# LSH attention with a soft MoE on one core: slot maxima joined by a reduce, and a new table of places

## The chip, the core and the metric

The kernel runs on one core of a Trainium2 chip. The metric is the device time of one execution in microseconds (us); of several runs the median counts. Before the change it is 492.49 us, the median of 3 runs (492.34 to 494.26).

## What is computed

```python
def _attn_ref(q, k, v, proj):                      # q, k, v: 4 x 8 x 768 x 64, proj: 64 x 6
    q_bits = (np.einsum('bhsd,dk->bhsk', q, proj) > 0)
    k_bits = (np.einsum('bhsd,dk->bhsk', k, proj) > 0)
    ...
    mask = q_bucket[:, :, :, None] == k_bucket[:, :, None, :]
    scores = np.where(mask, scale * np.matmul(q, k.transpose(0, 1, 3, 2)), -1e9)
    scores = scores - np.max(scores, axis=-1, keepdims=True)
    attn = np.exp(scores)
    attn = attn / (np.sum(attn, axis=-1, keepdims=True) + 1e-09)
    return np.matmul(attn, v)

def _moe_ref(x, phi, w1, w2):                      # x: 3072 x 512, 8 experts of 4 slots
    logits = x @ phi
    d = np.exp(logits - logits.max(0, keepdims=True))
    d /= d.sum(0, keepdims=True) + 1e-09
    slot_input = d.T @ x
    ...
    for e in range(E):
        slot_out[e] = np.maximum(slot_input[e] @ w1[e], 0.0) @ w2[e]
    c = np.exp(logits - logits.max(1, keepdims=True))
    c /= c.sum(1, keepdims=True) + 1e-09
    return c @ slot_out
```

The output of the attention, 4 batches of 768 rows with 8 heads side by side, is the x of the MoE. The softmax of its dispatch runs over all 3072 rows, so a running maximum and a running sum of each of the 32 slots go from batch to batch.

## The kernel before

There are 32 heads (4 batches of 8). Of each head, TensorE makes the raw scores twice. `smax` (L692) multiplies queries and keys for the row maxima, which VectorE takes from PSUM with `most` (L701, L704: 9 reductions of 128x512 a head) and turns into a shift (`shift`, L730 to L733) that a transpose and a small DMA put into the matrix XY (`shift_rows`, L740, L743, L600). `scores` (L755) then gives shifted scores, ScalarE makes exponents of them (`exps`, L761), GpSimd (POOL in the profile) adds the exponents up (`acc`, L769, L772), and TensorE multiplies them by v (`av`, L782: 24 matmuls a head, v from `load_v`, L578).

Two heads share one pair of loads (`load`, L484). Each pair is split into a rounded part on ScalarE (`split_hi`, L592, L609) and a rest on VectorE (`split_lo`, L596, two TENSOR_TENSOR of 128x768 a pair, both inputs in SBUF). The parts go to XY by DMAs of SyncE's queue (`spread_y`, `spread_bits`, `spread_l`, `spread_x`, all L600). The MoE's weights (w, L474, L476) come in by the same queue.

After the 8th head of a batch come its steps for the MoE. `batch_both` (L893 on ScalarE, L895 twice on GpSimd) adds two halves of the logits; `batch_max` (L906 to L914 on VectorE) makes the maximum of each slot over the batch; `batch_exp`, `batch_turn` and `batch_slots` (L961, 48 matmuls) weigh the rows; `batch_weigh` and `batch_share` (L995 to L1006) make the other softmax. In `batch_max` the tile `ml` has 64 partitions that matter: L906 takes each partition's maximum over 384 columns, L908 copies each half of 32 partitions beside the other, L909 joins the two, and L910 doubles the result to the partitions from 64 on.

The order is written by hand: tables give each step of each head a place. WHEN holds the places of an ordinary pair of heads, FIRST and LAST those at the two ends. A place is counted in slots, six to a head; steps are issued in order of their places, and each engine and each queue then takes its own instructions strictly in that order. All `batch_` steps have their places in WHEN as well, except for the last batch's.

What the change touches is these three tables and `batch_max`.

Of the kernel before, what the change touches and what calls it, by code (L numbers as in the profile page):

```python
# [76 lines left out]

FIRST = {('bits', 0): -69.9775,
 ('first_x', 0): -30.1551,
 ('first_x', 1): -25.0682,  # L80
 ('first_x', 2): -20.412,
 ('first_x', 3): -18.4961,
 ('load', 4, 0): -3.5217,
 ('load', 4, 1): -4.0427,
 ('bits', 2): -14.3602,
 ('split_hi', 2): -6.1587,
 ('split_lo', 2, 0): -4.0091,
 ('split_lo', 2, 1): -3.1985,
 ('spread_y', 2): -4.0649,
 ('spread_bits', 2): -3.553,  # L90
 ('spread_l', 2): 7.1875,
 ('spread_x', 2): 2.0822,
 ('smax', 1, 0, 0): -15.9674,
 ('smax', 1, 0, 1): -11.9944,
 ('smax', 1, 1, 0): -10.2152,
 ('smax', 1, 1, 1): -15.7053,
 ('smax', 1, 2, 0): -4.3906,
 ('smax', 1, 2, 1): -4.1302,
 ('smax', 1, 3, 0): -3.9981,
 ('smax', 1, 3, 1): -7.967,  # L100
 ('smax', 1, 4, 0): -3.8293,
 ('smax', 1, 4, 1): -5.0023,
 ('smax', 1, 5, 0): -4.8646,
 ('smax', 1, 5, 1): -9.7674,
 ('first_y', 1): -54.5168,
 ('first_y', 2): -17.6137,
 ('spread_y', 1): -27.3342,
 ('spread_l', 0): -18.6619,
 ('spread_bits', 1): -21.1518,
 ('bits_rest',): -37.973,  # L110
 ('bits_copy', 0): -66.7928,
 ('bits_copy', 1): -56.5144,
 ('first_w', 0, 0): -66.5811,
 ('first_w', 0, 1): -45.7928,
 ('copy_ident',): -27.8207,
 ('bits_out',): -12.7699,
 ('shift_first', 0): -19.1938,
 ('rows_first', 0): -18.4864,
 ('shift_first', 1): -13.5686,
 ('rows_first', 1): -12.6498,  # L120
 ('most', 1, 0): -13.0129,
 ('most', 1, 2): -10.1579,
 ('most', 1, 3): -12.9853,
 ('most', 1, 4): -3.8181,
 ('most', 1, 6): -3.2633,
 ('most', 1, 7): -6.0805,
 ('most', 1, 8): -3.0814,
 ('most', 1, 10): -4.6253,
 ('most', 1, 11): -9.4308,
 ('bits_first', 1): -46.476,  # L130
 ('split_hi', 0): -80.2217,
 ('split_lo', 0, 0): -30.0379,
 ('split_lo', 0, 1): -20.3056,
 ('spread_x', 0): -11.7196,
 ('load_v', 0): -22.952,
 ('smax', 0, 0, 0): -39.3574,
 ('scores', 0, 0, 0): -14.2041,
 ('most', 0, 0): -28.4376,
 ('exps', 0, 0): -11.531,
 ('smax', 0, 0, 1): -32.3847,  # L140
 ('scores', 0, 0, 1): -9.483,
 ('smax', 0, 1, 0): -31.1779,
 ('scores', 0, 1, 0): -8.3933,
 ('most', 0, 2): -23.5522,
 ('exps', 0, 2): -7.5483,
 ('smax', 0, 1, 1): -56.6523,
 ('scores', 0, 1, 1): -1.1034,
 ('most', 0, 3): -51.1186,
 ('exps', 0, 3): -0.8554,
 ('smax', 0, 2, 0): -33.7433,  # L150
 ('scores', 0, 2, 0): -12.1245,
 ('most', 0, 4): -25.3553,
 ('exps', 0, 4): -10.2628,
 ('smax', 0, 2, 1): -25.6195,
 ('scores', 0, 2, 1): -5.5845,
 ('smax', 0, 3, 0): -25.5483,
 ('scores', 0, 3, 0): -1.2874,
 ('most', 0, 6): -19.4151,
 ('exps', 0, 6): 1.0484,
 ('smax', 0, 3, 1): -26.0166,  # L160
 ('scores', 0, 3, 1): 0.5805,
 ('most', 0, 7): -23.0552,
 ('exps', 0, 7): 1.0692,
 ('smax', 0, 4, 0): -18.3291,
 ('scores', 0, 4, 0): -10.0448,
 ('most', 0, 8): -14.3729,
 ('exps', 0, 8): -7.9213,
 ('smax', 0, 4, 1): -23.8505,
 ('scores', 0, 4, 1): -4.5738,
 ('smax', 0, 5, 0): -21.0143,  # L170
 ('scores', 0, 5, 0): -2.6163,
 ('most', 0, 10): -18.7244,
 ('exps', 0, 10): -0.999,
 ('smax', 0, 5, 1): -20.7774,
 ('scores', 0, 5, 1): 1.5881,
 ('most', 0, 11): -17.8201,
 ('exps', 0, 11): 3.2827,
 ('av', 0, 0): -4.211,
 ('acc', 0, 1): 0.5901,
 ('av', 0, 1): 1.0472,  # L180
 ('acc', 0, 2): 3.7833,
 ('av', 0, 2): 2.6287,
 ('acc', 0, 3): 8.0943,
 ('av', 0, 3): 4.1871,
 ('acc', 0, 4): 9.2872,
 ('av', 0, 4): 4.819,
 ('acc', 0, 5): 12.8178,
 ('av', 0, 5): 9.3332,
 ('spread_l', 1): -14.0544,
 ('spread_x', 1): -13.7504,  # L190
 ('load_v', 1): -44.3971,
 ('scores', 1, 0, 0): 4.973,
 ('exps', 1, 0): 6.1018,
 ('scores', 1, 0, 1): 3.4362,
 ('scores', 1, 1, 0): 3.7635,
 ('exps', 1, 2): 4.5791,
 ('scores', 1, 1, 1): 3.0982,
 ('exps', 1, 3): 5.7775,
 ('scores', 1, 2, 0): 2.917,
 ('exps', 1, 4): 5.8263,  # L200
 ('scores', 1, 2, 1): 9.7364,
 ('scores', 1, 3, 0): 10.4691,
 ('exps', 1, 6): 10.964,
 ('scores', 1, 3, 1): 5.8015,
 ('exps', 1, 7): 8.512,
 ('scores', 1, 4, 0): 5.3574,
 ('exps', 1, 8): 6.9816,
 ('scores', 1, 4, 1): 10.0245,
 ('scores', 1, 5, 0): 11.0987,
 ('exps', 1, 10): 12.5989,  # L210
 ('scores', 1, 5, 1): 8.2291,
 ('exps', 1, 11): 10.001,
 ('shift', 1): 0.0971,
 ('shift_rows', 1): 0.888,
 ('av', 1, 0): 10.6213,
 ('acc', 1, 1): 12.6345,
 ('av', 1, 1): 10.7441,
 ('acc', 1, 2): 13.2627,
 ('av', 1, 2): 11.6349,
 ('acc', 1, 3): 15.0399,  # L220
 ('av', 1, 3): 11.8759,
 ('acc', 1, 4): 19.4341,
 ('av', 1, 4): 14.7303,
 ('acc', 1, 5): 19.5025,
 ('av', 1, 5): 15.0341,
 ('load', 2, 0): -29.7899,
 ('load', 2, 1): -48.8868,
 ('load_v', 2): 14.3982,
 ('smax', 2, 0, 0): -0.6141,
 ('scores', 2, 0, 0): 11.2906,  # L230
 ('most', 2, 0): 1.9018,
 ('exps', 2, 0): 11.4754,
 ('smax', 2, 0, 1): 1.3301,
 ('scores', 2, 0, 1): 16.8442,
 ('smax', 2, 1, 0): 2.1038,
 ('scores', 2, 1, 0): 17.3813,
 ('most', 2, 2): 4.5992,
 ('exps', 2, 2): 17.9432,
 ('smax', 2, 1, 1): 3.4166,
 ('scores', 2, 1, 1): 13.5684,  # L240
 ('most', 2, 3): 6.6254,
 ('exps', 2, 3): 13.9228,
 ('smax', 2, 2, 0): 5.3372,
 ('scores', 2, 2, 0): 13.5443,
 ('most', 2, 4): 6.8467,
 ('exps', 2, 4): 16.2233,
 ('smax', 2, 2, 1): -0.0995,
 ('scores', 2, 2, 1): 11.5208,
 ('smax', 2, 3, 0): 1.5951,
 ('scores', 2, 3, 0): 12.5714,  # L250
 ('most', 2, 6): 2.9705,
 ('exps', 2, 6): 13.4436,
 ('smax', 2, 3, 1): 3.1284,
 ('scores', 2, 3, 1): 12.9678,
 ('most', 2, 7): 6.2017,
 ('exps', 2, 7): 14.722,
 ('smax', 2, 4, 0): 2.6343,
 ('scores', 2, 4, 0): 17.8316,
 ('most', 2, 8): 4.6871,
 ('exps', 2, 8): 17.9065,  # L260
 ('smax', 2, 4, 1): 5.4192,
 ('scores', 2, 4, 1): 15.908,
 ('smax', 2, 5, 0): 5.9488,
 ('scores', 2, 5, 0): 16.8341,
 ('most', 2, 10): 7.5949,
 ('exps', 2, 10): 17.5487,
 ('smax', 2, 5, 1): 7.6679,
 ('scores', 2, 5, 1): 16.4966,
# [1072 lines left out]
```

## Time and profile before

| what | value |
|---|---|
| median of 3 runs | 492.49 us |
| the profiled execution | 493.42 us, its span 491.8 us |
| instructions | 10961 |
| granted TensorE clock, mean | 0.979 of full speed |

The profile is of one execution. Its page gives for each engine the busy time, for each stretch the busy share and the granted clock of TensorE (2.4 GHz is 1.0, 1.2 GHz is 0.5), the chain of work that ended last, and groups of instructions by line. The queries on the trace give single instructions in order of time, with the idle time in front of each and what ended it in square brackets. PE is TensorE, DVE VectorE, ACT ScalarE, POOL GpSimd, SPq the queue of DMAs that SyncE issues.

### The profile page before, as it was taken

To read this page: it belongs to the slowest core of one execution; us is meant where nothing else is said; L and a number is where in the kernel's file an instruction comes from. 1 tells how busy PE (TensorE), PEld (TensorE's weight loads), DVE (VectorE), ACT (ScalarE), POOL (GpSimd) and SP (SyncE) were. 2 spreads that over 40 slices of the span, in tenths; PEclk is the share of its full clock that TensorE was granted. 3 is DMA by queue.
4 is the path that set the end of the run, shared out by engine and by line. 5 is a ranking of instruction groups with operands and counts; after the bars stand their busy time and mean duration, and the time that the engine had idled before them with its cause. 6 is when DMAs were issued, how large, how long until landed. Compare 5 with 4: busy or idle time off the path is not lost.

```text
span 491.8 us, 10961 instructions
## 1 busy us (share of the span) xinstructions
PE 455.0 (93%) x4159; PEld 286.3 (58%) x4159; DVE 374.0 (76%) x680; ACT 271.7 (55%) x569; POOL 332.7 (68%) x209
## 2 busy tenths in 40 slices
...
GB/s 181 168 151 141 126 224 143 212 135 229 136 221 59 179 178 181 175 181 178 182 124 112 188 142 202 164 194 100 170 43 155 46 163 319 365 379 301 413 361 258
DMA packets 37703, 93.20 MB, mean 190 GB/s; under 512 B 7106, under 2 KB 13380, under 8 KB 37652
## 3 DMA queue, kind: packets, MB, share of 16 engines
...
q14 instruction: 18, 0.15, 0.1%
...
HBM read 52.76 MB, written 6.29 MB: 120 GB/s over the span
## 4 chain that ended last, share of the span: by engine, by line
PE 65%; DMA 13%; DVE 9%; SPq 8%; issue 2%; ACT 1%; DVEq 0%; ACTq 0%
PE st L755 22%; PE av L782 15%; PE smx L692 12%; SPq L600 7%; DMA v<-vt 6%; DMA XY<-w 5%; PE qs L1255 3%; PE qh L1202 3%; DVE ml L909 3%; DVE mx L704 2%; DVE w L596 2%; PE mi L794 2%; PE mi L639 2%; PE mi L819 1%; ACT w L592 1%
## 5 line engine op out<-in xcount | busy, mean ns | idle before, releaser
L772 POOL TENSOR_TENSOR acc<-acc,pt 128x768 f32<-128x768 f32 x125 | 236.4, 1900 | 42.6 <-ACT pt L761 37.6
L761 ACT ACTIVATE pt<-st 128x512 f32<-128x512 f32 x288 | 156.9, 591 | 50.0 <-PE st L755 44.4
L755 PE MATMUL st<-XY 128*128 128x256 f32 (+1 forms) x768 | 176.6, 347 | 0.1
L704 DVE TENSOR_REDUCE mx<-smx 128x1 f32<-128x512 f32 x192 | 129.6, 687 | 36.1 <-PE smx L692 35.3
L782 PE MATMUL av<-pt,v 128*32 128x384 f32 x1536 | 135.3, 488 | 6.1 <-DMA v<-vt 4.6
L755 PEld LDWEIGHTS st<-XY 128*128 128x128 f32 x768 | 126.7, 194 | 20.9 <-issue 5.3
L692 PE MATMUL smx<-XY 96*128 96x256 f32 (+1 forms) x384 | 120.2, 367 | 18.1 <-DVE mx L704 14.4
L692 PEld LDWEIGHTS smx<-XY 96*128 96x128 f32 x384 | 69.5, 195 | 46.0 <-DVE mx L704 22.1
L782 PEld LDWEIGHTS av<-pt,v 128*32 128x32 f32 x1536 | 46.9, 110 | 79.0 <-issue 62.6
L701 DVE TENSOR_REDUCE mx<-smx 128x2 f32<-128x512 f32 x96 | 65.9, 687 | 5.9 <-PE smx L692 4.9
L769 POOL TENSOR_TENSOR acc<-pt 128x768 f32<-128x768 f32 x32 | 58.8, 1837 | 9.2 <-ACT pt L761 5.3
L786 ACT COPY avs<-av 128x384 f32<-128x384 f32 x32 | 15.4, 481 | 59.4 <-PE av L782 59.4
L596 DVE TENSOR_TENSOR w<-raw,w 128x768 fp32r<-128x768 f32 x28 | 37.8, 1351 | 9.9 <-ACT w L592 9.8
L592 ACT CAST w<-raw 128x768 fp32r<-128x768 f32 x30 | 23.7, 833 | 12.6 <-DMA XY<-mr 5.3
L609 ACT CAST XY<-w 64x768 fp32r<-64x768 f32 x30 | 23.5, 833 | 0.1
L797 ACT ACTIVATE sm<-mi,eps 128x384 f32<-128x384 f32 x15 | 8.7, 582 | 19.9 <-PE mi L794 19.9
L842 DVE TENSOR_TENSOR xq<-mi,r 128x384 f32<-128x384 f32 x30 | 16.7, 558 | 2.2
L841 DVE STREAM_TRANSPOSE mi<-avs 128x384 f32<-128x384 f32 x30 | 17.6, 586 | 0.5
L895 POOL TENSOR_TENSOR dl<-lacc,dl 64x384 f32<-64x384 f32 x6 | 7.8, 1304 | 14.2 <-issue 14.0
L996 POOL TENSOR_TENSOR lacc<-sm,cm 128x192 f32<-128x192 f32 x3 | 1.5, 510 | 23.1 <-DVE cm L995 23.1
L1255 PE MATMUL qs<-w 128*32 128x128 f32 x464 | 15.5, 274 | 0.4 <-issue 0.4
L811 ACT COPY r<-rt 64x12 f32<-64x12 f32 x60 | 12.0, 200 | 6.2 <-DVE rt L803 5.5
(174 smaller groups left out, 366.3 us busy)
## 6 DMA issues: line engine op xcount, KB each, us to landing
...
```

What stands on the lines that cost most here:

```text
L592: nc.scalar.copy(st[h]["w4"][:, 2 * x], st[h]["raw", x])
L596: (nc.vector if h > 2 else nc.gpsimd).tensor_tensor(out=w[:, 2 * x + 1], in0=st[h]["raw", x], in1=w[:, 2 * x], op=ALU.subtract)
L600: eng.dma_start(out=dst.bitcast(F32), in_=src.bitcast(F32))
L692: nc.tensor.matmul(pt[:, o:o + b - a], s["Y"][0:96, 0, t * P:(t + 1) * P], s["Y"][0:96, 1, a:b], start=True, stop=True)
L701: nc.vector.tensor_reduce(out=mx[:, n - 1:n + 1], in_=s["sm_ps", n - 1].rearrange("p (a x) -> p a x", a=2), axis=AX.X, op=ALU.max)
L704: nc.vector.reduce_max(out=mx[:, n:n + 1], in_=s["sm_ps", n], axis=AX.X)
L755: nc.tensor.matmul(pt[:, o:o + b - a], x[:, 1, i * P:(i + 1) * P], x[:, 0, a:b], start=first, stop=not first)
L761: nc.scalar.activation(s["P", n // 4][:, 512 * u:512 * u + 512], s["st_ps", n - (n % 4 == 2)], AF.Exp, scale=D ** -0.5)
L769: nc.gpsimd.tensor_tensor(out=s["acc"], in0=pr[:, 0:S], in1=pr[:, S:2 * S], op=ALU.add)
L772: eng.tensor_tensor(out=s["acc"], in0=s["acc"], in1=pr[:, a * S:(a + 1) * S], op=ALU.add)
L782: nc.tensor.matmul(s["av"][2 * e + 32 * c:2 * e + 32 * c + 32, 0:HC], s["v"][:, i, e:e + 32], pr[:, o + c * HC:o + (c + 1) * HC], start=(i ...
L1255: nc.tensor.matmul(pos[i][32 * j:32 * j + 32, 0:w], hTs[g][:, f, 32 * j:32 * j + 32], wt[1, x, 2 * g + f // 4, j][:, (f % 4) * HM + o:(f % ...
```

## The change

In `batch_max` the tile `ml` gets a fourth column, the first result goes to column 0 (`mo`), its copy from the other half to column 1 (`sw`), and L909 becomes a TENSOR_REDUCE over these two neighbouring columns instead of a TENSOR_TENSOR of one column with the other. All numbers of the tables are new, so all steps have other places; no step is added or left out.

```diff
-WHEN = {'load': -21.761,
- 'bits': -14.953,
- 'bits_over': -14.2535,
- 'split_hi': -12.6082,
- 'split_lo': [-11.9997, -11.2616],
- 'spread': [[-11.7311, -11.8254, -10.8277, -7.598], [-10.8259, -11.7635, -11.5808, -10.4552]],
- 'load_v': [0.1314, 2.3531],
...
- 'av': [[8.8176, 9.1545, 9.4692, 9.5265, 9.5397, 9.7898], [5.9962, 6.0054, 6.1722, 6.2052, 6.3699, 6.3882]],
...
- 'batch_both': 23.58,
- 'batch_max': 25.0983,
...
+WHEN = {'load': -17.7191,
+ 'bits': -14.4811,
+ 'bits_over': -14.4231,
+ 'split_hi': -11.8329,
+ 'split_lo': [-11.0358, -8.8327],
+ 'spread': [[-11.1688, -7.9572, -7.1212, -4.9753], [-9.4418, -9.0048, -8.9766, -8.3581]],
+ 'load_v': [0.8254, 0.8377],
...
+ 'av': [[9.338, 9.6759, 9.8253, 9.848, 9.9231, 9.9801], [6.073, 6.1257, 6.303, 6.4394, 6.7221, 7.1612]],
...
+ 'batch_both': 21.828,
+ 'batch_max': 24.3,
...
     def batch_max(b):
         z = bst[b]
-        ml = dp.tile([P, 3], F32, name="ml", bufs=1)
-        mb, sw, z["lb"] = (ml[:, n:n + 1] for n in range(3))
+        ml = dp.tile([P, 4], F32, name="ml", bufs=1)
+        mo, sw, mb, z["lb"] = (ml[:, n:n + 1] for n in range(4))
         z["al"] = dp.tile([P, 1], F32, name="al", bufs=1)
         z["nm"], z["om"] = run_n[b % 2], run_n[1 - b % 2]
-        nc.vector.reduce_max(out=mb[0:64], in_=logits_of(b)[0:64], axis=AX.X)
+        nc.vector.reduce_max(out=mo[0:64], in_=logits_of(b)[0:64], axis=AX.X)
         for x in range(2):
-            nc.vector.tensor_copy(sw[32 * x:32 * x + 32], mb[32 - 32 * x:64 - 32 * x])
-        nc.vector.tensor_tensor(out=mb[0:64], in0=mb[0:64], in1=sw[0:64], op=ALU.max)
+            nc.vector.tensor_copy(sw[32 * x:32 * x + 32], mo[32 - 32 * x:64 - 32 * x])
+        nc.vector.reduce_max(out=mb[0:64], in_=ml[0:64, 0:2], axis=AX.X)
         nc.vector.tensor_copy(mb[64:128], mb[0:64])
```

What the new tables do is seen in the order on the engines. The first place is VectorE at the end of the first batch, around `batch_max` (L906 to L912). Of the names, smx are raw scores in PSUM, w the split pair, raw its load, ml the maxima. Before:

```order
L704 TENSOR_REDUCE mx<-smx 128x1
L596 TENSOR_TENSOR w_1701<-raw_1481,w_1701 128x768
L704 TENSOR_REDUCE mx<-smx 128x1 x2
L596 TENSOR_TENSOR w_1701<-raw_1483,w_1701 128x768
L841 STREAM_TRANSPOSE mi<-avs 128x384
L842 TENSOR_TENSOR xq<-mi,r 128x12x32
L906 TENSOR_REDUCE ml<-dl 64x1
L908 COPY ml<-ml 32x1 x2
L909 TENSOR_TENSOR ml<-ml 64x1
L910 COPY ml<-ml 64x1
L912 TENSOR_SCALAR run_n_124<-ml 128x1
L704 TENSOR_REDUCE mx<-smx 128x1
```

And with the change:

```order
L704 TENSOR_REDUCE mx<-smx 128x1
L906 TENSOR_REDUCE ml<-dl 64x1
L908 COPY ml<-ml 32x1 x2
L909 TENSOR_REDUCE ml<-ml 64x1
L910 COPY ml<-ml 64x1
L912 TENSOR_SCALAR run_n_124<-ml 128x1
L704 TENSOR_REDUCE mx<-smx 128x1
L596 TENSOR_TENSOR w_1718<-raw_1497,w_1718 128x768
L704 TENSOR_REDUCE mx<-smx 128x1
L841 STREAM_TRANSPOSE mi<-avs 128x384
L842 TENSOR_TENSOR xq<-mi,r 128x12x32
L596 TENSOR_TENSOR w_1718<-raw_1499,w_1718 128x768
```

`batch_max` now stands ahead of both L596, and the second L596 stands behind L841 and L842 instead of ahead of them, in this pair and in the others.

The second place is SyncE's queue of DMAs in one ordinary pair of heads. XY<-w, XY<-bt and XY<-mr are the parts, bits and shifts that go to XY, v_103 is the v of the pair's second head. Before:

```order
L484 DMA raw_1187<-qk 128x768
L484 DMA raw_1189<-qk 128x768
L474 DMA w<-w 128x1024
L600 DMA XY_152<-mr 1x12x128
L600 DMA XY_153<-w_1113 64x2x768
L600 DMA XY_153<-w_1113 32x2x768
L600 DMA XY_151<-bt 13x384 x2
L600 DMA XY_151<-bt 12x384 x2
L600 DMA XY_151<-w_1113 32x2x768
L600 DMA XY_151<-w_1113 64x2x768 x2
L600 DMA XY_151<-w_1113 32x2x768
L578 DMA v_103<-vt 128x384
```

And with the change:

```order
L484 DMA raw_1203<-qk 128x768
L484 DMA raw_1205<-qk 128x768
L578 DMA v_103<-vt 128x384
L600 DMA XY_152<-mr 1x12x128
L600 DMA XY_153<-w_1126 64x2x768
L600 DMA XY_153<-w_1126 32x2x768
L600 DMA XY_151<-w_1126 64x2x768
L600 DMA XY_151<-bt 13x384 x2
L600 DMA XY_151<-bt 12x384 x2
L600 DMA XY_151<-w_1126 32x2x768
L600 DMA XY_151<-w_1126 64x2x768
L600 DMA XY_151<-w_1126 32x2x768
```

The load of v_103 went from behind the shift and the ten transfers to XY to ahead of all of them, and the weight piece (w<-w) that stood ahead of the shift went elsewhere.

## Rows read from the trace of the kernel before

**Rows 1.** The page: busy time of each engine, share of the span, instructions.

```profile
PE 455.0 (93%) x4159; PEld 286.3 (58%) x4159; DVE 374.0 (76%) x680; ACT 271.7 (55%) x569; POOL 332.7 (68%) x209
```

**Rows 2.** Stretches: length, busy time by engine, granted clock; first ordinary pairs, then batch pairs.

```profile
core 0: us, PE busy (x) PEld busy (x) DVE busy (x) ACT busy (x) POOL busy (x), PEclk, DMA share, GB/s
64.88:89.06 24.18, 23.11 (x192) 14.42 (x192) 20.66 (x37) 15.21 (x32) 18.93 (x10) 1.00 0.69 185
...
89.06:114.14 25.08, 24.36 (x199) 15.24 (x197) 20.91 (x38) 15.09 (x32) 18.92 (x10) 1.00 0.65 171
...
138.33:169.77 31.44, 27.32 (x246) 17.23 (x245) 28.34 (x52) 17.30 (x40) 21.21 (x17) 0.89 0.53 141
169.77:194.69 24.92, 24.41 (x202) 15.24 (x204) 20.50 (x36) 15.09 (x32) 21.46 (x11) 1.00 0.65 174
...
243.06:275.02 31.96, 27.12 (x241) 17.20 (x234) 28.38 (x50) 17.67 (x41) 21.21 (x18) 0.89 0.52 141
275.02:300.97 25.95, 24.69 (x205) 15.08 (x208) 22.19 (x37) 15.21 (x32) 21.72 (x13) 1.00 0.64 166
300.97:326.34 25.37, 23.86 (x198) 14.54 (x194) 20.55 (x36) 15.07 (x32) 18.92 (x10) 1.00 0.68 184
...
350.75:381.65 30.90, 25.95 (x240) 16.13 (x233) 28.25 (x50) 17.53 (x41) 21.13 (x17) 0.94 0.42 104
```

**Rows 3.** Line L909: durations in ns, least, median, most.

```profile
L909 DVE TENSOR_TENSOR ml<-ml x4: 150/4286/4301, 143.4 to 439.5; 64x1 f32<-64x1 f32 x4
```

**Rows 4.** Timeline of VectorE at the end of the first batch: start, us, what.

```profile
142.54 0.53 DVE L906 TENSOR_REDUCE ml<-dl 64x1 f32<-64x384 f32 x1
...
143.44 4.30 DVE L909 TENSOR_TENSOR ml<-ml 64x1 f32<-64x1 f32 x1
147.77 0.15 DVE L910 COPY ml<-ml 64x1 f32<-64x1 f32 x1
```

**Rows 5.** Timeline of GpSimd there: the run, and its first instruction alone.

```profile
142.36 9.15 POOL L772 TENSOR_TENSOR acc<-acc,pt 128x768 f32<-128x768 f32 x5
142.36 1.84 POOL L772 TENSOR_TENSOR acc<-acc,pt 128x768 f32<-128x768 f32 x1
```

**Rows 6.** Timeline of TensorE: its first matmul after L909, in three batches.

```profile
148.76 0.80 PE L692 MATMUL smx<-XY 96*128 96x512 f32 x1 [4.12 <-DVE mx L704]
253.53 0.80 PE L692 MATMUL smx<-XY 96*128 96x512 f32 x1 [4.30 <-DVE mx L704]
361.23 0.57 PE L692 MATMUL smx<-XY 96*128 96x512 f32 x1 [4.31 <-DVE mx L704]
```

**Rows 7.** Stretches behind these idle times, columns as in rows 2.

```profile
148.76:153.00 4.24, 4.24 (x12) 3.47 (x13) 2.43 (x6) 2.32 (x6) 2.68 (x2) 0.50 0.02 4
253.53:257.80 4.27, 4.27 (x12) 3.50 (x13) 2.45 (x7) 2.49 (x7) 2.62 (x2) 0.50 0.00 0
361.23:365.00 3.77, 3.77 (x11) 3.05 (x12) 2.43 (x6) 2.49 (x7) 2.61 (x2) 0.55 0.00 0
```

**Rows 8.** Groups by line: a small reduction from SBUF, and the batch's matmuls.

```profile
L730 DVE TENSOR_REDUCE mi<-mx 128x6 f32<-128x12 f32 x31 | 5.4, 174 | 1.2
L961 PE MATMUL mi<-xq,avs 64*32 64x256 f32 x144 | 4.6, 380 | 0.0
```

**Rows 9.** Waits of TensorE on transfers: us, times, longest.

```profile
PE av L782 <- DMA v<-vt: 4.6, 6, 1.5
PE smx L692 <- DMA XY<-w: 2.1, 3, 1.1
```

**Rows 10.** The chain that ended last, 183 to 195 us: start, us, what.

```profile
183.49 0.78 SPq L600
...
189.51 4.94 DMA v<-vt
...
194.49 4.24 PE av L782 x48
```

**Rows 11.** Line L596: durations in ns, least, median, most.

```profile
L596 DVE TENSOR_TENSOR w<-raw,w x28: 946/1111/2643, 41.7 to 383.7; 128x768 fp32r<-128x768 f32 x28
```

More of the change, by code (lines that the diff above doesn't have):

```diff
@@ L78 @@
[L78 to L268, printed above, removed]
- ('most', 2, 11): 7.9367,
- ('exps', 2, 11): 17.4186,
- ('shift', 2): 8.4183,
- ('shift_rows', 2): 9.9591,
- ('spread_y', 3): 4.7545,
- ('spread_bits', 3): 4.2903,
- ('spread_l', 3): 4.3609,
- ('spread_x', 3): 9.1174}
@@ new lines @@
+WHEN = {'load': -17.7191,
[5 more added lines that the diff above has]
+ 'load_v': [0.8254, 0.8377],
+ 'smax': [[-5.5404, -5.239, -5.1892, -3.4795, -4.556, -5.0483, -4.843, -3.5583, -2.8991, -3.0436, -2.9566, -3.1005], [-7.8798, -7.8794, -7.7178, -7.0216, -6.4263, -3.51, -3.3611, -6.2386, -3.9477, -1.0552, -0.461, -1.6316]],
+ 'scores': [[4.5609, 7.21, 7.364, 3.906, 4.1133, 6.8372, 6.8451, 6.2517, 8.5061, 6.9378, 8.0448, 6.0827], [2.8461, 3.0229, 3.0899, 2.7306, 5.4216, 2.8842, 3.1016, 3.0901, 4.3757, 5.5889, 5.6987, 4.4733]],
+ 'shift': [-2.121, 0.7267],
+ 'shift_rows': [-2.0058, 0.8441],
+ 'acc': [[9.0875, 9.7174, 9.8785, 12.1896, 12.6158], [6.3062, 7.7947, 7.9479, 8.6485, 9.2388]],
+ 'av': [[9.338, 9.6759, 9.8253, 9.848, 9.9231, 9.9801], [6.073, 6.1257, 6.303, 6.4394, 6.7221, 7.1612]],
+ 'pair_sum': 21.1732,
+ 'pair_turn': 21.4204,
+ 'pair_rec': 21.5496,
+ 'pair_log': 21.2289,
+ 'pair_x': [22.4828, 26.9143],
+ 'pair_add': 21.7661,
+ 'batch_both': 21.828,
+ 'batch_max': 24.3,
+ 'batch_exp': 25.8514,
+ 'batch_turn': 31.2612,
+ 'batch_scale': 55.916,
+ 'batch_slots': 31.8942,
+ 'batch_weigh': 33.0293,
+ 'batch_share': 33.1062,
+ 'batch_arrange': 33.3142,
+ 'load_weights': 4.0141,
+ 'most': [[-4.8818, -4.7863, -3.2084, -4.2595, -4.7244, -3.3546, -2.6678, -2.668, -3.0405], [-6.6845, -5.8069, -5.7203, -5.3984, 0.5832, -4.0729, -0.1428, 0.6825, 0.6173]],
+ 'exps': [[6.4986, 7.4445, 5.9862, 5.6311, 6.9383, 6.6245, 8.7147, 8.1519, 6.6135], [3.0047, 4.4676, 2.8329, 5.7431, 3.8883, 3.889, 5.4944, 6.2149, 6.3]]}
```

456 lines of the change are left out of this document (317 added, 139 removed).

## The prediction

> **What bounds the kernel now.** I read the page first: TensorE is busy 93% of the span, VectorE 76%, GpSimd 68% [rows 1]. Then I cut the span at the first L596 of each pair of heads into 13 pairs, nearly the whole attention. Most ordinary pairs take 24.2 us, with TensorE busy for 23.1 to 24.2 and VectorE for 20.7, which leaves VectorE 24.18 - 20.66 = 3.52 us of slack [rows 2]. So in an ordinary pair TensorE is the limit. Three pairs stand out: those with the end of a batch in them take 31.44, 31.96 and 30.90 us at a mean clock of 0.89, 0.89 and 0.94 [rows 2], though a batch adds only 48 matmuls to TensorE, 4.6 us for three batches [rows 8]. The timeline shows why. L909, a maximum of 64x1 with 64x1, takes 4.3 us in these batches and 0.15 in the last one [rows 3]. VectorE can free no PSUM buffer of raw scores meanwhile, and TensorE stands still for 4.12, 4.30 and 4.31 us [rows 6]. After each of these its granted clock is 0.50, 0.50 and 0.55 for some 4 us, mostly the 1.2 GHz level [rows 7].
>
> Why is L909 slow? When it begins, GpSimd has just started five additions back to back, 9.15 us in all; L909 begins at 143.44 and ends at 147.74, after more than two of them [rows 4, 5]. The last batch's L909, at 439.5, is behind all additions of GpSimd, and takes 0.15 [rows 3]. L906, a reduction with one SBUF input, lies wholly beside the first of the five additions and takes 0.53; the copy L910 takes 0.15 inside the run [rows 4, 5]. What singles L909 out is two inputs from SBUF. L596 has two as well, and takes 0.95 at best and 2.64 at worst [rows 11].
>
> This agrees with the Trainium skill, SBUF — State Buffer, Who interferes with whom: a VectorE instruction with two SBUF inputs contends with a GpSimd instruction that reads SBUF, a tensor_reduce on trn2 never does, and the loser waits until the other has finished. In length the trace differs: one addition ends 0.76 us after L909 began (142.36 + 1.84 - 143.44, [rows 4, 5]), so by the rule L909 would have taken about 0.9 us, and it took 4.30. The measurement decides; the rule returns at the last rival.
>
> **The change, part by part.**
>
> L909 as a reduction over two columns. The trace has no 64x1 from 64x2. Bounds: 0.17 us, the reduction of 128x12 in SBUF [rows 8], and 4.30, what it replaces [rows 3]. I take 0.17, because L906 and L730 are reductions that read SBUF, as the new one does. The four copies and scalings around it stay.
>
> The Trainium skill, VectorE: DVE Perf Modes, Rules for kernel authors, speaks against the change: tensor_reduce is the slowest operation of VectorE and is to be restructured away on a hot path. At this size the rows show 0.17 beside an undisturbed 0.15, so by rule and row the sum would differ by 0.02 us a batch.
>
> What a batch pair gains. Three estimates. (a) Straight: the idle time, 4.12 + 4.30 + 4.31 = 12.73 [rows 6], and what the low clock cost, 4.24 x 0.50 + 4.27 x 0.50 + 3.77 x 0.45 = 5.95 [rows 7]; 18.7. (b) By TensorE: an ordinary 24.18 plus 1.53 of batch matmuls is 25.7 a pair; the three take 94.30 now [rows 2], so 94.30 - 77.1 = 17.2. (c) By VectorE: its busy time in the three pairs less L909 and plus 0.17 is 24.21, 24.27 and 24.13 [rows 2, 4]; if each pair keeps all the 3.52 of slack that an ordinary one has, they take 83.2, a gain of 11.1. I take the mean of the three, **15.7**, since in the stretches of low clock VectorE is busy only 2.4 of 4 us [rows 7], so both engines gave away time; 11.1 and 18.7 stay as ends.
>
> The load of v. A few pairs take longer than 24.18: 25.08, 24.92, 25.95 and 25.37, together 4.6 us [rows 2]. The chain of waits shows what happens in them: SyncE's queue issues transfers to XY one after another, 0.78 us for one, comes to v at 189.51, v lands 4.94 us later, and the matmuls av begin at 194.49 [rows 10]. TensorE waits 4.6 us in six such places, and 2.1 in three for XY [rows 9]. The change puts the v of the second head ahead of the shift and ten transfers to XY. In the table its lead over its matmul goes from 5.996 - 2.353 = 3.64 slots to 6.073 - 0.838 = 5.24; with 24.18 / 12 = 2.0 us a slot, from 7.3 to 10.6 us. I count the share of v, 4.6 x 4.6 / 6.7 = **3.2**; ends 0 and 6.7. The price: the shift and the transfers come one issue later, 0.78 us; against it a weight piece is no longer ahead of the shift. The move of the keys' part of XY for the second head now precedes its bits, which helps the three waits on XY; I count that at nothing.
>
> The L596. The second one moves behind L841 and L842, and both go behind `batch_max` in a batch pair. If the first, mostly free now, met an addition as the second does, it would cost 28 / 2 = 14 times 1.85 - 0.95 = 12.6 us of VectorE, 0.9 a pair. The cover is the 3.52 of slack a pair, and while they run TensorE has 4.2 us of av matmuls, which wait for no reduction [rows 10]. So nothing; were the cover gone, 12.6.
>
> `batch_max` ahead of L596. L906 waits for GpSimd's additions of the logits. `batch_both` goes from 23.58 to 21.83 slots, `batch_max` from 25.10 to 24.30, so the distance between them grows from 1.5 to 2.5 slots, 3.0 to 5.0 us. Behind a waiting L906 stand the reductions that free raw scores, and TensorE waits for these. I cost it at nothing; a wait as long as the old stall would bring back 4.3 of idle time a batch.
>
> The two ends. FIRST and LAST are new too; the same work stays there. Nothing, no better than 2 us either way, about half of TensorE's waits on v.
>
> **Sum:** 493.42 - 15.7 - 3.2 = 474.5 for an execution like the profiled one. That one is 0.9 us above the median of 492.49, so the median comes to **473.6**.
>
> **The rivals.**
>
> 1. VectorE becomes the bound in the batch pairs, and the new order hides no transfer: 492.5 - 11.1 = 481. For it: 24.2 us of VectorE work in a pair that TensorE could do in 25.7. Against: VectorE waited there too [rows 7]. Chance 0.14.
>
> 2. The new order also tightens the ordinary pairs, whose TensorE is busy for 23.1 of 24.18 [rows 2]: half of that 1.1 in the ten ordinary pairs is 5.4 more, 468. Against: the pairs are near their limit. Chance 0.10.
>
> 3. The change doesn't do what it says: the stall is no matter of the second input, and the reduction over two columns takes 4.3 as well. Only v is gained: 492.5 - 3.2 = 489. Against it L906 and L910 [rows 4]. Chance 0.06.
>
> 4. Slower: the stall moves from L909 to L596. In the new order an L596 comes upon a run of additions on GpSimd and waits, as L909 did, through several of them, 4.15 us more than alone; with two L596 in a pair the slack is used up and the cover of av may not reach. One event of that kind cost a batch pair 15.7 / 3 = 5.2 us. The gain of 18.9 is gone at the fourth event in 14 pairs; at four or five, some 495. For it: at worst L596 took 2.64 already, and L909's 4.3 shows that a wait can last longer than one addition. Against: no L596 took so long in 28 [rows 11]. Since one L909 after the other waited through several additions, I leave it 0.08. By the rule of the Trainium skill, SBUF — State Buffer, named above, an L596 would wait for one addition at most, which av covers, and this rival would have no chance at all; the length of L909 speaks against it.
>
> **How the numbers follow.** Forecast 0.62, with 467 to 481 from its own ends (492.5 - 18.7 - 6.7 and 492.5 - 11.1); rivals 0.14, 0.10, 0.06, 0.08. A measurement of this kernel tells about 0.5% from no change, 2.5 us, so faster means under 490.0. Forecast, 1 and 2 give 0.86; of rival 3 half lies under it, 0.03: faster 0.89. Same: the other half of 3 and 0.02 of 4, 0.05. Slower 0.06. The range of 466 to 484 takes in these ends, rivals 1 and 2 and some 2 us for the two ends of the program, and leaves out 3 and 4.
>
> **What would show it.** L909 at 0.15 to 0.2 us in all four batches. No idle time of TensorE near 4 us around it, and no stretch at 0.50 behind it. Batch pairs of 26 to 28 us, ordinary ones at 24.2 or a little less. Waits of av on v near nothing. Wrong it would be with L909 still at 4 us, with L596 longer than 2.7, with L906 waiting for GpSimd, or with new idle time of TensorE in the ordinary pairs.

## The result, and the profile after

The changed kernel takes 472.98 us, the median of 4 runs (469.70 to 473.32), against 492.41 for the kernel before, 4 runs beside it (492.33 to 494.26). The ratio is 0.9582, with a 95% interval of 0.9534 to 0.9630. The forecast was 473.6. The profiled execution took 473.32, its span is 471.5.

The page's line of busy times answers to [rows 1]: TensorE's share went from 93 to 96%, at nearly the same busy time.

```profile
PE 452.6 (96%) x4159; PEld 284.8 (60%) x4159; DVE 358.1 (76%) x680; ACT 277.2 (59%) x569; POOL 342.2 (73%) x209
```

L909 answers to [rows 3]: durations in ns, least, median, most. It is 0.15 us in all four batches. The line of L596 below it answers to [rows 11].

```profile
L909 DVE TENSOR_REDUCE ml<-ml x4: 146/147/147, 139.3 to 417.8; 64x1 f32<-64x2 f32 x4
...
L596 DVE TENSOR_TENSOR w<-raw,w x28: 948/1272/2380, 45.3 to 364.2; 128x768 fp32r<-128x768 f32 x28
```

VectorE's timeline at the end of the first batch answers to [rows 4]:

```profile
138.40 0.54 DVE L906 TENSOR_REDUCE ml<-dl 64x1 f32<-64x384 f32 x1
...
139.31 0.15 DVE L909 TENSOR_REDUCE ml<-ml 64x1 f32<-64x2 f32 x1
...
140.34 1.49 DVE L596 TENSOR_TENSOR w<-raw,w 128x768 fp32r<-128x768 f32 x1
...
143.44 0.95 DVE L596 TENSOR_TENSOR w<-raw,w 128x768 fp32r<-128x768 f32 x1
```

And GpSimd's, which answers to [rows 5]:

```profile
135.19 2.09 POOL L895 TENSOR_TENSOR dl<-lacc,dl 64x384 f32<-64x384 f32 x2 [5.34 <-ACT dl L893]
137.25 3.77 POOL L772 TENSOR_TENSOR acc<-acc,pt 128x768 f32<-128x768 f32 x2
140.97 2.55 POOL L769 TENSOR_TENSOR acc<-pt 128x768 f32<-128x768 f32 x1
```

The reduction, from 139.31 to 139.46, lies wholly inside a run of two additions, and is not held up. L906 has no idle time in front of it: L895 had ended at 137.28, so the longer distance of `batch_max` was enough. The first L596 now meets an addition and takes 1.49; the second, free, takes 0.95. That is the other way round than before.

Pairs of heads, cut as in [rows 2] at the first L596 of each, columns as there: an ordinary pair, then the three with the end of a batch.

```profile
68.92:92.52 23.60, 23.54 (x198) 14.95 (x194) 20.41 (x36) 15.54 (x32) 19.66 (x11) 1.00 0.69 188
...
140.34:165.75 25.41, 24.84 (x238) 15.51 (x234) 22.78 (x45) 17.04 (x39) 23.01 (x18) 1.00 0.64 171
237.75:262.94 25.19, 24.89 (x238) 15.47 (x234) 22.82 (x45) 17.06 (x40) 22.94 (x18) 1.00 0.63 170
334.96:360.25 25.29, 24.89 (x238) 15.49 (x234) 22.87 (x46) 17.06 (x40) 23.02 (x18) 1.00 0.53 132
```

A batch pair fell from some 31.4 to 25.3 us and its clock is 1.00 throughout. An ordinary pair fell from 24.18 to 23.60, and TensorE is busy for all but 0.06 of it.

TensorE's waits (us, times, longest) answer to [rows 9]. The wait on v went from 4.6 to 0.5, and that on XY<-w is gone. The wait on the maxima, which held the stalls, was this before:

```profile
PE smx L692 <- DVE mx L704: 14.4, 5, 4.3
```

With the change it is small, 2.5 us on L704 and 1.3 on L701:

```profile
PE smx L692 <- DVE mx L704: 2.5, 6, 0.6
...
PE smx L692 <- DVE mx L701: 1.3, 2, 0.8
...
PE av L782 <- DMA v<-vt: 0.5, 1, 0.5
...
PE st L755 <- DMA XY<-mr: 0.2, 1, 0.2
```

The two ends became longer. Up to the first L596 of a pair, and from the last such on, the kernel before shows these stretches:

```profile
0.00:41.73 41.73, 39.58 (x260) 26.54 (x260) 27.40 (x57) 24.25 (x40) 32.53 (x25) 1.00 0.63 159
381.65:491.80 110.15, 97.43 (x1258) 62.24 (x1256) 54.66 (x116) 44.74 (x103) 46.66 (x33) 0.98 0.81 291
```

and the changed one these:

```profile
0.00:45.28 45.28, 40.90 (x251) 26.74 (x252) 28.44 (x58) 24.20 (x41) 29.60 (x23) 0.96 0.63 163
...
360.25:471.50 111.25, 99.44 (x1249) 61.94 (x1241) 54.76 (x114) 44.76 (x102) 46.48 (x32) 0.97 0.79 286
```

So the gain of this execution's span, 491.8 - 471.5 = 20.3 us, has four parts:

| stretch | before | after | gain |
|---|---|---|---|
| start, to the first L596 | 41.73 | 45.28 | -3.55 |
| ten ordinary pairs | 245.6 | 239.1 | +6.6 |
| three batch pairs | 94.3 | 75.9 | +18.4 |
| end, from the last pair's first L596 | 110.2 | 111.2 | -1.1 |

Two things bear on how this table is read. In the new order `batch_max` stands ahead of the first L596, and so lies in the pair in front, which the table counts as ordinary. With these three pairs taken in, the six pairs around the ends of batches went from 167.1 to 148.2 us, a gain of 19.0, and the other seven gained 6.0. And in each of the two ends this one execution has a stretch at a granted clock of 0.50:

```profile
24.30:27.60 3.30, 3.30 (x16) 1.98 (x9) 0.72 (x2) 0.49 (x2) 0.79 (x1) 0.50 0.27 60
420.30:423.60 3.30, 3.30 (x48) 2.08 (x31) 1.31 (x5) 0.61 (x2) 0.00 (x0) 0.50 0.69 236
```

The last kernel of the experiments has the same FIRST and LAST, and its profiled execution has neither of the two: its start takes 44.02 us at a clock of 1.00, and its end 110.36.

```profile
364.14:474.50 110.36, 97.88 (x1249) 61.54 (x1241) 54.76 (x114) 44.69 (x102) 46.45 (x32) 0.98 0.80 288
```

So of the 4.65 us that the two ends lost, some 2.5 are seen without a low clock, nearly all of them in the start.

### The profile page after: what moved, and what is told of

It is laid out like the page before. It is cut to its first block, busy times and chain, and to the rows that moved or that the text cites. A ratio compares the mean times of both kernels' runs of the same rounds, so it can differ in the third digit from the quotient of the medians.

```text
span 471.5 us, 11017 instructions
## 1 busy us (share of the span) xinstructions
PE 452.6 (96%) x4159; PEld 284.8 (60%) x4159; DVE 358.1 (76%) x680; ACT 277.2 (59%) x569; POOL 342.2 (73%) x209
## 4 chain that ended last, share of the span: by engine, by line
PE 78%; DVE 9%; DMA 7%; issue 2%; SPq 1%; ACT 1%; DVEq 0%; POOL 0%; ACTq 0%
PE st L755 25%; PE av L782 20%; PE smx L692 14%; DVE w L596 3%; PE qs L1255 3%; PE qh L1202 3%; DVE mx L704 3%; DMA v<-vt 2%; PE mi L794 2%; PE mi L639 2%; PE mi L819 2%; DMA w<-w 1%; SPq L600 1%; PE mi L740 1%; DMA fold<-cst 1%
## 5 line engine op out<-in xcount | busy, mean ns | idle before, releaser
L772 POOL TENSOR_TENSOR acc<-acc,pt 128x768 f32<-128x768 f32 x125 | 246.4, 1977 | 7.6 <-ACT pt L761 1.0
L761 ACT ACTIVATE pt<-st 128x512 f32<-128x512 f32 x288 | 160.3, 595 | 55.8 <-PE st L755 52.6
L704 DVE TENSOR_REDUCE mx<-smx 128x1 f32<-128x512 f32 x192 | 130.6, 688 | 20.3 <-PE smx L692 17.0
L692 PE MATMUL smx<-XY 96*128 96x512 f32 (+1 forms) x384 | 116.0, 361 | 4.5 <-DVE mx L704 2.5
L692 PEld LDWEIGHTS smx<-XY 96*128 96x128 f32 x384 | 67.9, 190 | 36.4 <-DVE mx L704 15.8
L769 POOL TENSOR_TENSOR acc<-pt 128x768 f32<-128x768 f32 x32 | 61.1, 1908 | 32.1 <-ACT pt L761 31.9
L701 DVE TENSOR_REDUCE mx<-smx 128x2 f32<-128x512 f32 x96 | 65.7, 685 | 9.2 <-PE smx L692 8.5
L596 DVE TENSOR_TENSOR w<-raw,w 128x768 fp32r<-128x768 f32 x28 | 39.4, 1407 | 6.2 <-ACT w L592 5.6
L801 DVE STREAM_TRANSPOSE sm<-sm 128x384 f32<-128x384 f32 x15 | 8.7, 577 | 13.8 <-ACT sm L797 13.8
L842 DVE TENSOR_TENSOR xq<-mi,r 128x384 f32<-128x384 f32 x30 | 16.7, 558 | 2.1
L841 DVE STREAM_TRANSPOSE mi<-avs 128x384 f32<-128x384 f32 x30 | 17.4, 579 | 1.1 <-ACT mr L743 1.1
L895 POOL TENSOR_TENSOR dl<-lacc,dl 64x384 f32<-64x384 f32 x6 | 6.0, 1008 | 16.3 <-ACT dl L893 16.1
```

The source lines that it names most:

```text
L596: (nc.vector if h > 2 else nc.gpsimd).tensor_tensor(out=w[:, 2 * x + 1], in0=st[h]["raw", x], in1=w[:, 2 * x], op=ALU.subtract)
L692: nc.tensor.matmul(pt[:, o:o + b - a], s["Y"][0:96, 0, t * P:(t + 1) * P], s["Y"][0:96, 1, a:b], start=True, stop=True)
L701: nc.vector.tensor_reduce(out=mx[:, n - 1:n + 1], in_=s["sm_ps", n - 1].rearrange("p (a x) -> p a x", a=2), axis=AX.X, op=ALU.max)
L704: nc.vector.reduce_max(out=mx[:, n:n + 1], in_=s["sm_ps", n], axis=AX.X)
L761: nc.scalar.activation(s["P", n // 4][:, 512 * u:512 * u + 512], s["st_ps", n - (n % 4 == 2)], AF.Exp, scale=D ** -0.5)
L769: nc.gpsimd.tensor_tensor(out=s["acc"], in0=pr[:, 0:S], in1=pr[:, S:2 * S], op=ALU.add)
```

## The experiments

Each kernel was timed in rounds beside the kernel before. Medians of several sessions are told with the median of before in the same session (492.12 for the first four, 492.56 for the next four, 492.51 and 494.36 for the last two).

### The reduction alone

The tables of before, with the new `batch_max`; of its lines the join is shown, and the fourth column of `ml` comes with it:

```diff
...
-        nc.vector.tensor_tensor(out=mb[0:64], in0=mb[0:64], in1=sw[0:64], op=ALU.max)
+        nc.vector.reduce_max(out=mb[0:64], in_=ml[0:64, 0:2], axis=AX.X)
```

> The old tables with the new L909 alone. Theory: the stall of L909 is worth 15.7 us (ends 11.1 and 18.7), so 476.7 us, between 473.7 and 481.3, L909 at 0.15 us, and no idle time of TensorE near 4 us. Rival: the new places bring the gain and the reduction is a detail; then no more than 3 us are gained, 489 or above.

Measured: 473.47 us (471.12 to 477.04), ratio 0.9632 (0.9574 to 0.9689), 0.2 below the forecast range. The three batch pairs:

```profile
137.01:162.31 25.30, 25.20 (x243) 15.26 (x242) 23.98 (x51) 17.17 (x40) 21.29 (x17) 1.00 0.66 179
235.55:260.78 25.23, 24.52 (x239) 14.89 (x232) 23.98 (x50) 17.36 (x41) 21.22 (x17) 1.00 0.66 177
334.67:359.91 25.24, 24.69 (x240) 14.98 (x237) 24.01 (x50) 17.35 (x41) 21.23 (x17) 1.00 0.52 127
```

They sum to 75.77, a gain of 94.30 - 75.77 = 18.5. This edit of `batch_max` alone is worth as much as the whole change, within what a measurement tells. TensorE is busy for 24.5 to 25.2 of 25.3 and VectorE for 24.0: VectorE has 1.3 us of idle time left in a pair, not the 3.5 of an ordinary one.

### The places alone

The new tables, with the TENSOR_TENSOR of before in L909 and the three columns of `ml`:

```diff
...
-        nc.vector.reduce_max(out=mb[0:64], in_=ml[0:64, 0:2], axis=AX.X)
+        nc.vector.tensor_tensor(out=mb[0:64], in0=mb[0:64], in1=sw[0:64], op=ALU.max)
```

> The new tables with the old L909 (a maximum of two SBUF inputs). Theory A, the instruction is what counts: L909 waits for several additions again, three stalls of 4.3 us come back, and the time is 15.7 us above the change, near 488.7. Theory B, the new place is enough: in the changed kernel L909 stands 0.3 us into the second of two additions, and behind that one the next waits for other engines, so L909 would wait some 1.7 us, ahead of 4 us of av matmuls that need no reduction; the time is then that of the change plus 0 to 4 us, 473 to 477. I hold B likelier, 0.6.

Measured: 478.89 us (476.83 to 480.25), ratio 0.9734 (0.9691 to 0.9776). The TENSOR_TENSOR takes 1.71 here, not 4.3. VectorE, then GpSimd:

```profile
137.67 1.71 DVE L909 TENSOR_TENSOR ml<-ml 64x1 f32<-64x1 f32 x1
```

```profile
135.62 3.75 POOL L772 TENSOR_TENSOR acc<-acc,pt 128x768 f32<-128x768 f32 x2
139.33 1.83 POOL L769 TENSOR_TENSOR acc<-pt 128x768 f32<-128x768 f32 x1
```

It ends at 139.38, with the second of the two additions. So the parts don't add up: by medians the reduction alone gives 492.12 - 473.47 = 18.7, the places alone 13.2, both together 19.4. Most of what the places give alone is the same stall, shortened: in the profiles the six pairs around the ends of batches take 155.3 us instead of 167.1. Theory B had the length of L909, but its time, 473 to 477, came out 2 us too low; TensorE still stood idle for 1.1 us in each of the three batches.

### The load of v ahead, in the old tables

The kernel with the reduction alone, and the second head's v ahead of the shift and the transfers to XY:

```diff
- 'load_v': [0.1314, 2.3531],
+ 'load_v': [0.1314, -2.33],
```

> As the old tables with the new L909, and the load of the second head's v moved in the table from 2.3531 to -2.33, which puts it ahead of the shift and the ten transfers to XY, nothing else. Theory: the late v is what the odd heads gain by. In the changed kernel the steps of nine odd heads from the end of one av to the next are 0.7 to 1.7 us shorter, 10.5 us together; so this run is 10 us (7 to 12) below the run with the new L909 alone, near 467. By the term of the forecast it is 3.2 below. Rival: the odd heads gain by the other moves, and this run is within 1.5 us of the run with the new L909 alone.

Measured: 474.72 us (472.59 to 475.56), ratio 0.9644 (0.9611 to 0.9677): no gain over 473.47. TensorE's waits on transfers:

```profile
PE st L755 <- DMA XY<-mr: 4.5, 5, 1.2
...
PE av L782 <- DMA v<-vt: 1.3, 1, 1.3
```

With the reduction alone these were 1.0 and 3.0. The wait was not removed, it moved from v to the shift behind v.

### The join by another instruction

The tables of before, L909 as a TENSOR_SCALAR whose scalar is the second column, read from SBUF for each partition; the fourth column of `ml` comes with it:

```diff
...
-        nc.vector.tensor_tensor(out=mb[0:64], in0=mb[0:64], in1=sw[0:64], op=ALU.max)
+        nc.vector.tensor_scalar_max(mb[0:64], mo[0:64], sw[0:64])
```

> The old tables, with L909 as a TENSOR_SCALAR: one column as the tensor input, the other as its scalar per partition. It tells what kind of second input makes the stall. Theory: only a second tensor input from SBUF competes with GpSimd, so L909 takes 0.15 to 0.25 us and the time equals that of the run with the reduction, within 0.5%. Rival: any second operand from SBUF waits, L909 takes 4.3 us, and the time is that of the kernel before, 492.

Measured: 475.71 us (473.71 to 476.15), ratio 0.9663 (0.9632 to 0.9694).

```profile
L909 DVE TENSOR_SCALAR ml<-ml x4: 205/205/205, 143.4 to 420.0; 64x1 f32<-64x1 f32 x4
```

No stall, though it reads the same two columns. Of the two forms, only the second input as a tensor waits for GpSimd.

### The old tables at the two ends

The changed kernel with FIRST of before, with LAST of before, and with both.

```diff
-FIRST = {('bits', 0): -72.6747,
+FIRST = {('bits', 0): -69.9775,
...
```

> The changed kernel with the table FIRST of before. Theory A (the new places win in the odd heads and give it back at the two ends): the end of head 0 comes at about 37 us instead of 41.9, heads 2 to 4 some 3.4 us earlier, and the time falls by 3 to 5 us under the changed kernel, to 468 to 470; the odd heads keep their 7.3 us a step. Rival B (the start only shifts a wait that the next pairs hide anyway): head 0 ends earlier, but by head 8 nothing is left, and the time stays at 473.

> The changed kernel with the table LAST of before. Theory A: the stretch behind the end of head 29 falls from 83.7 to 81.5 to 82 us, and the time by about 2, to 471. Rival B: the end is set by what the pairs before it leave behind, and the stretch stays at 83.7, the time at 473.

> The changed kernel with FIRST and LAST of before, so that only WHEN and the reduction are new. Theory A (the two ends each cost what the head-by-head table shows, and add up): 466 to 468 us, faster than the changed kernel and than the reduction in the old tables (473.5). Rival B (the odd heads' gain is lost elsewhere): 471 to 473.

Measured: 473.73 (471.78 to 477.27), 473.62 (472.39 to 477.49) and 473.88 us (472.08 to 477.41, 6 runs). None is faster than the changed kernel. The start and the end of the third:

```profile
0.00:42.21 42.21, 40.12 (x268) 26.40 (x268) 28.21 (x59) 24.69 (x41) 33.44 (x25) 1.00 0.66 172
359.15:470.20 111.05, 99.32 (x1249) 61.69 (x1241) 54.62 (x114) 44.35 (x102) 46.44 (x32) 0.97 0.80 287
```

The start came back to 42.21, but the ten ordinary pairs then took 241.2 instead of 239.1, the first of them 25.04 instead of 23.64. The end stayed at 111.1, though its table is the old one, but it again has a stretch at a clock of 0.50 (418.6 to 421.5). The run with LAST alone of before has none there, and its end is short:

```profile
361.10:470.50 109.40, 97.97 (x1249) 61.35 (x1241) 54.59 (x114) 44.36 (x102) 46.45 (x32) 0.98 0.81 291
```

In that run too the ten ordinary pairs take 241.2. So my theory A, by which what an end gives back comes off the time, is wrong: the pairs took it up, and which of their steps do so was not looked at. The numbers of a pair and those of the ends belong together, and the balance stays within what can be measured.

### What sets the length of L909: one addition moved

The kernel before, TENSOR_TENSOR in L909 and all, with one place changed; then the same place at another value.

```diff
- 'acc': [[7.6023, 9.3544, 10.6138, 11.3951, 12.4712], [3.4667, 6.2743, 8.31, 8.3711, 8.826]],
+ 'acc': [[7.6023, 9.3544, 10.6138, 11.3951, 11.5], [3.4667, 6.2743, 8.31, 8.3711, 8.826]],
```

> The kernel before, with its TENSOR_TENSOR in L909, where one place is changed: the last addition of the even head (acc, 12.4712 to 11.5 slots) goes ahead of L895, so that the additions behind L895 come in another grouping. Theory A (how long L909 waits hangs on how the additions behind it stand, since the places-only kernel had 1.7 us with another grouping): L909 takes 0.8 to 1.9 us, and the time falls by 8 to 12 us, to 480 to 484. Rival B (L909 waits for any run of additions in these tables to its end or its third end): L909 stays at 4.2 to 4.4 us and the time at 492.

```diff
- 'acc': [[7.6023, 9.3544, 10.6138, 11.3951, 12.4712], [3.4667, 6.2743, 8.31, 8.3711, 8.826]],
+ 'acc': [[7.6023, 9.3544, 10.6138, 11.3951, 11.62], [3.4667, 6.2743, 8.31, 8.3711, 8.826]],
```

> The kernel before, with its TENSOR_TENSOR in L909, where the last addition of the even head has its place at 11.62 slots instead of 12.4712: it now stands directly behind the second L895, ahead of the two of the other head, so that GpSimd goes through 101, 99, 99, 99, 99 instead of 99, 101, 99, 99, 99 (numbers of acc). It is the one addition of the run that waits for no semaphore; L909 should come while it is running. Theory A (what goes past a waiting L909 is an addition that waits for no semaphore, and the one behind it): nothing can go past, L909 takes 0.7 to 0.9 us, the time is 475 to 477. Rival B (L909 has to wait while additions of two heads follow one another without a gap, however they wait): it waits through the first two, 2.5 to 2.7 us, the time is 482 to 486. Rival C (any interleaving of two heads in the run costs the whole 4.3): 4.3 us, 492.

Measured: 475.66 us (474.40 to 478.60), ratio 0.9688 (0.9643 to 0.9732), for the first, and 486.77 (485.76 to 487.74), ratio 0.9877 (0.9825 to 0.9929), for the second. In the first, where all additions behind L895 belong to one head, VectorE and GpSimd show:

```profile
142.59 0.77 DVE L909 TENSOR_TENSOR ml<-ml 64x1 f32<-64x1 f32 x1
```

```profile
141.53 1.82 POOL L772 TENSOR_TENSOR acc<-acc,pt 128x768 f32<-128x768 f32 x1
...
143.43 1.82 POOL L772 TENSOR_TENSOR acc<-acc,pt 128x768 f32<-128x768 f32 x1
```

The first addition ends at 143.35, the next, which needs its result, begins at 143.43. L909 ends at 143.36, in this gap of 0.08. Theory A had the length nearly right, and a time 4 us too high. In the second kernel, where an addition of one head goes ahead of those of the other:

```profile
144.49 2.52 DVE L909 TENSOR_TENSOR ml<-ml 64x1 f32<-64x1 f32 x1
```

```profile
143.41 1.83 POOL L772 TENSOR_TENSOR acc<-acc,pt 128x768 f32<-128x768 f32 x1
...
145.20 1.80 POOL L772 TENSOR_TENSOR acc<-acc,pt 128x768 f32<-128x768 f32 x1
...
147.08 1.82 POOL L772 TENSOR_TENSOR acc<-acc,pt 128x768 f32<-128x768 f32 x1
```

The second addition begins at 145.20, before the first has ended (145.24). The third begins 0.08 after the second's end at 147.00. L909 ends at 147.01, in the first gap that there is. That is what rival B expected of the run, with a time 0.8 us above its range, and theory A (an addition without a wait goes past) is wrong. In the kernel before, the run is one addition of the one head between two of the other:

```profile
142.36 5.37 POOL L772 TENSOR_TENSOR acc<-acc,pt 128x768 f32<-128x768 f32 x3
...
147.81 1.81 POOL L772 TENSOR_TENSOR acc<-acc,pt 128x768 f32<-128x768 f32 x1
```

The gap comes behind the third addition, from 147.73 to 147.81, and L909 ends in it, at 147.74. The other two batches of these three kernels show the same. The three batch pairs together follow the length of L909:

| kernel (old tables) | L909, us | three batch pairs, us |
|---|---|---|
| reduction alone | 0.15 | 75.8 |
| join by TENSOR_SCALAR | 0.21 | 76.1 |
| addition ahead of L895 | 0.77 | 77.9 |
| addition directly behind L895 | 2.53 | 87.1 |
| before | 4.29 | 94.3 |

### When L909 comes

The places-only kernel with `batch_max` half a slot later:

```diff
- 'batch_max': 24.3,
+ 'batch_max': 24.8,
```

> The places-only kernel (new tables, L909 still a TENSOR_TENSOR) with batch_max at 24.8 slots instead of 24.3, so that one more reduction L704 goes ahead of L906 and L909 comes some 0.7 us later, in the second half of the addition that it met at its start. The additions behind it are the same: L769 follows without a gap. Theory A (what decides is when L909 comes: at the very start of an addition it gets in at that addition's end, later it has to wait for a gap on GpSimd): L909 waits through L769 and further, over 2.8 us in at least two of three batches, and the time rises by 4 us or more over the 478.9 of the places-only kernel. Rival B (what decides is the addition that follows: L769 lets L909 in, L772 without a gap does not): L909 takes about 1.0 us, ends with the running addition, and the time is 476 to 479.

Measured: 478.29 us (476.31 to 481.20), ratio 0.9707 (0.9615 to 0.9799). L909 takes 1.00 in each of the three batches:

```profile
138.71 1.00 DVE L909 TENSOR_TENSOR ml<-ml 64x1 f32<-64x1 f32 x1
```

```profile
139.66 1.84 POOL L769 TENSOR_TENSOR acc<-pt 128x768 f32<-128x768 f32 x1
```

It gets in at the end of the running addition, 139.70, though L769 has begun at 139.66, without a gap. The moment at which it comes does not decide, as rival B had it. Why L909 gets in ahead of this L769 and not ahead of the additions in the runs of the section before is not settled. In these tables the addition that L909 meets has a gap of 0.08 in front of it (137.79 to 137.87 here), in the others it follows L895 without one; no run separates that from the difference between L769 and L772.

L596, the large instruction with two SBUF inputs, needs no gap at all. In the places-only kernel it begins beside the L769 shown there, which runs from 139.33 to 141.16 and has no gap on either side:

```profile
140.26 1.71 DVE L596 TENSOR_TENSOR w<-raw,w 128x768 fp32r<-128x768 f32 x1
```

```profile
141.13 2.54 POOL L772 TENSOR_TENSOR acc<-acc,pt 128x768 f32<-128x768 f32 x1
```

L596 gets in at the end of that addition, and the next one, already begun, shows 2.54 instead of 1.83. In the twelve profiles the longest of 336 L596 takes 2.64, less than one addition and its own 0.95 together. Why the tiny L909 waits longer than the large L596 is open.

## Why the prediction was right or wrong

The total was right, 473.6 against 472.98, but with terms that erred on both sides, and that they cancel this closely is luck. By the parts of the profile the batch pairs gave 2.7 us more than forecast and the ordinary pairs 3.4 more, and the ends took 4.65.

**The cause of the stall** was read rightly. The reduction alone takes it away, and so does another form with one tensor input. The Trainium skill, SBUF — State Buffer, Who interferes with whom, names this pair of instructions, and the runs agree with it on who waits. They differ on how long: by its rule, read as in the prediction, the wait ends with the running instruction, and here it ended there only in some runs (0.77, 1.00 and 1.71) and behind a second or third addition in others (2.53 and 4.30).

**The reduction, 15.7.** The term was too small: 18.5 from the batch pairs with the reduction alone, 18.7 by medians. Estimate (a), 18.7, was right, and the step that failed was to average it with (c), 11.1. That one supposed that a batch pair keeps the 3.52 us of VectorE's slack that an ordinary pair has. It keeps 1.3: that slack was what TensorE's limit left over and not a need of VectorE's. Estimate (b), an ordinary pair and TensorE's batch matmuls on top, forecast 25.7 a pair; they take 25.3.

**The load of v, 3.2.** The mechanism was half right. In the new tables the waits on v and on XY fell from 6.7 us to 0.7, near the upper end that I gave. But v ahead of the shift is not what does it alone: in the old tables it gains nothing, and TensorE waits 4.5 us for the shift. The step that failed is the price, "the shift and the transfers come one issue later, 0.78 us", and its counterweight, "a weight piece is no longer ahead of the shift", which that run didn't have. The new tables move the weights, the shift and the XY transfers as well; which of these carries the gain was not tried apart.

**The ordinary pairs.** They gained 6.6 in all, of which 2.6 also come with the reduction alone, whose ten ordinary pairs take 243.0 in its profile. The term for v was to come out of these pairs, so 3.4 are beyond the forecast. Rival 2 had this mechanism, at 5.4 on top, and TensorE now fills 23.54 of 23.60 in the pair shown.

**The two ends, nothing.** Wrong: they lost 3.55 and 1.1, outside the 2 us either way. I had taken "the same work stays there" for the same time. In the start the clock is 0.96 instead of 1.00 and TensorE is idle for 45.28 - 40.90 = 4.4 us instead of 2.2. Some 2 us of the loss belong to stretches of low clock that another execution with the same two tables does not have; the rest, nearly all in the start, is still above the 2 us. The 4.65 took back most of the 6.1 that I had counted too little in the terms above.

**L596 and `batch_max`, nothing.** Right. The collision went from the second L596 to the first, the longest is 2.38, no more than a wait for one addition, and TensorE's waits on the maxima fell to 2.5 and 1.3 us. With that rivals 1 and 4 fell; VectorE has 2.4 us to spare in a batch pair and 2.8 in the pair in front, where `batch_max` now lies.

**That the places and the reduction are separate terms** was assumed without being said. The places alone shorten L909 from 4.3 to 1.7 and gain 13.2 us. In the new tables the reduction is worth only 478.89 - 472.98 = 5.9.

No version tried is measurably faster than the changed kernel; the reduction in the old tables equals it.
